# Holding back two kinds of transfer on one DMA queue until a unit's turned inputs are issued

## The chip, the cores and the metric

The kernel runs on one core of one Trainium2 chip. The metric is the time of one execution in device microseconds (us): the median of three runs. Beside it there is one execution taken by the hardware profiler, from which the trace and all its rows come.

## The reference

The reference applies the same two layers twice to one sequence of 2048 tokens with 576 channels, in bf16.

```python
def _layernorm(x, axis=-1, eps=1e-5):
    m = jnp.mean(x, axis=axis, keepdims=True)
    v = jnp.var(x, axis=axis, keepdims=True)
    return (x - m) / jnp.sqrt(v + eps)
...
    def _A_ref(q, k, v, shift_k, ssm_k, ssm_D):
...
        for t in range(ks):                      # ks = 4 taps
            k_shift = k_shift + k_pad[:, t:t + S, :] * shift_k[:, ks - 1 - t][None, None, :]
        kv = k_shift * v
...
        y = y + kv * ssm_D[None, None, :]        # y: causal convolution of kv with the filter ssm_k, by FFT
        return q * y

    def _B_ref(x, w_gate, w_up, w_down):
        return (_gelu(x @ w_gate) * (x @ w_up)) @ w_down

    x = A_q
    x = x + _A_ref(_layernorm(x, axis=-1), A_k, A_v, A_shift_k, A_ssm_k, A_ssm_D)
    x = x + _B_ref(_layernorm(x, axis=-1), B_w_gate, B_w_up, B_w_down)
    x = x + _A_ref(_layernorm(x, axis=-1), A_k, A_v, A_shift_k, A_ssm_k, A_ssm_D)
    x = x + _B_ref(_layernorm(x, axis=-1), B_w_gate, B_w_up, B_w_down)
    return x
```

The hidden width of the feed-forward layer B is 4608. The convolution's result y does not depend on x, so it is computed once and used in both layers A, where it multiplies the normed x (the gate).

## The kernel before

**Units and passes.** The 2048 tokens are four chunks of 512. A unit is one feed-forward layer on one chunk. There are eight, in this order: units 0 and 1 are the first layer on chunks 0 and 1, units 2 and 3 the second layer on chunks 0 and 1, units 4 to 7 the same on chunks 2 and 3. Passes over the weights hold the units [0], [1, 2], [3, 4], [5, 6], [7]. Each pass goes through the hidden width in three phases of 1536 columns, and in a phase it visits its units one after the other. A visit is 216 gate/up matmuls (line 1581; unit 0's first visit uses line 1506) with a GELU on ACT (line 1585) and a product on DVE (line 1586), and then 96 down matmuls (line 1601) in four accumulators, one for each block of 128 tokens. DVE adds these to the residual `x_c` (lines 1632 and 1637). Three buffers of PSUM serve gate/up pairs and down accumulators alike.

**A unit's input.** The gate/up matmuls need the normed x turned, channels on partitions: the tile `xnT`. For each block of 128 tokens a normed tile `xn` is made, on DVE (`norm_v`, lines 1265 and 1267) or on ACT (`norm`, line 1257), and put on the list `xn_made` with the time at which the planner expects it. `spreads` takes it from there and issues two DMA transposes from SP's queue (`spread`, line 1290), which write the block's columns of `xnT`. `xn_done[ui]` counts a unit's blocks; a unit has `RT` = 4. For unit 1 the norms of blocks 0, 2 and 3 are made on DVE, that of block 1 on ACT; for units 2 to 7 all are made on ACT. The small steps of each norm run on POOL (lines 1185, 1200, 1201, 1205) and its sum of squares on ACT (line 1193). `nq` holds norms that ACT is still to make.

**Weights.** Gate and up weights come in groups of four blocks of 128 hidden columns, three buffers (`load_wgu`, lines 1147 to 1149: three transfers on SP's queue), down weights in halves of a phase, three buffers (`load_wd`, line 1157, SP too). `when_due` puts a load with its due time on the list `due`; `weights` issues what is on it.

**The convolution beside it.** The class `Conv` computes y for chunks 2 and 3 while the units run. Its filter is turned first: `turn(b)` issues four DMA transposes of the filter from DRAM, one at a time, on SP's queue (line 429, tile `hb`), and later a write of the turned chunk to DRAM from POOL's queue (line 434, `Td`). `filt(b)` loads it from there (POOL, line 448, tile `hT`) and transforms it (PE line 289, ACT line 292, DVE lines 252 to 265). `step(b)` loads k and v for the chunk (POOL, lines 171 and 176), forms their product with the taps (DVE, lines 189 to 199), transforms it and multiplies. All these loads stand on one list, `conv.L`, which is worked off in its order by `run_loads`: `turn(2)`, `turn(3)`, `filt(2)` and its `step`, and so on. A piece of a turn is held for as long as `conv.turning()` is true.

**The order.** The program is written out in one pass over the visits, with a planner's clock: `t.pe`, `t.act` and `t.dve` are expected times. Between two pairs of gate/up matmuls, and between down matmuls, `fill` is called. It calls `weights`, then `conv.run_loads`, then `spreads`, and after these gives DVE, ACT, POOL and PE the steps of convolution and norms that fit the time left. What is issued on an engine stays in this order. SP's queue therefore carries weights, filter turns and the turns of `xnT` in the order in which `fill` came to them, and an entry that waits holds the ones behind it.

The test that holds weights back is in `weights`, and the one that holds the filter's turns is set just ahead of the visits:

```python
            near = (xn_made or nq) and xn_done.get(1, 0) < RT
            if near and due[0][0] > t.pe + HOLD:
                break
...
        conv.tight, conv.turning = chained, lambda: bool(xn_made or nq)
```

`HOLD` is 14 us. `nq` is filled only by norms that ACT makes, and `xn_made` is empty again as soon as `spreads` has issued what it holds.

Of the kernel before, what the change touches and what calls it, by code (L numbers as in the profile page):

```python
# [26 lines left out]
RT = BS // P  # L27
# [1062 lines left out]
def ssm_geglu_kernel(ctx, tc, A_q, A_k, A_v, A_shift_k, A_ssm_k, A_ssm_D, B_x, B_w_gate, B_w_up,  # L1090
# [45 lines left out]
    conv = Conv(spare, tc, ctx, t, A_k, A_v, A_shift_k, A_ssm_k, A_ssm_D, ident, psp, cpsp, ypool)  # L1136
# [32 lines left out]
    aq, nq = deque(), deque()  # L1169
# [115 lines left out]
    xn_made = deque()  # L1285
# [14 lines left out]
    xnT_of, xn_done = {}, {}  # L1300
# [32 lines left out]
    def when_due(when, load, n):  # L1333
        due.append((when, len(due), load, n))
        due.sort(key=lambda d: d[0])

    def weights():

        while due:
            near = (xn_made or nq) and xn_done.get(1, 0) < RT  # L1340
            if near and due[0][0] > t.pe + HOLD:
                break
            _, _, load, n = due.pop(0)
            load(n)
# [6 lines left out]
    def fill(limit, tensor, conv_first):  # L1351
        weights()
        conv.run_loads()
        spreads()
        while True:
            if conv_first:
                if not (conv.run_v(limit) or run_vq(limit)):
                    break
            else:
                done = run_vq(limit)  # L1360
                if done is None or not (done or conv.run_v(limit)):
                    break
        while run_aq(min(limit, t.pe + 2.3)):
            pass
        conv.flush(t.pe)
        if tensor and (hurry() or t.pe > conv.last + (CHAINED if chained() else 0.0)):
            for _ in range(3):
                if not conv.run_p():
                    break

    with tc.manual_schedule():
# [155 lines left out]
        def wanted():  # L1527
            need = vq[0][0] if vq else (None,)
            kind = conv.Pq[0][3] if conv.Pq and len(conv.Pq[0]) > 3 else None
            if isinstance(kind, tuple):  # L1530
                return kind[1:] >= LATE
            return kind is not None and need[0] == "y2" and need[1:3] not in conv.y_at
        now = lambda: wanted() or hurry() and (t.pe > 60.0 or conv.fresh > 0)
        conv.tight, conv.turning = chained, lambda: bool(xn_made or nq)
        visits = []
        for pi, us in enumerate(passes):
            visits += [(pi * NP + ph, ph, ui, k == 0, k == len(us) - 1)
# [1 line left out]
        for wb, ph, ui, first, final in visits:  # L1539
# [17 lines left out]
            if first and wb > 0:  # L1557
                when_due(t.pe + FP * C_GU, load_wd, 2 * wb + 1)
                when_due(t.pe + FP * C_GU + 35.0, load_wd, 2 * wb + 2)
            weights()  # L1560
            xnT = xnT_of[ui]
            end = ph == NP - 1
# [81 lines left out]
@with_exitstack  # L1644
def kernel(
    ctx: ExitStack,
    tc: tile.TileContext,
    A_q: bass.AP,
    A_k: bass.AP,
    A_v: bass.AP,  # L1650
    A_shift_k: bass.AP,
    A_ssm_k: bass.AP,
    A_ssm_D: bass.AP,
    B_x: bass.AP,
    B_w_gate: bass.AP,
    B_w_up: bass.AP,
    B_w_down: bass.AP,
    out: bass.AP,
):
    ssm_geglu_kernel(tc, A_q, A_k, A_v, A_shift_k, A_ssm_k, A_ssm_D, B_x, B_w_gate, B_w_up,  # L1660
                     B_w_down, out)
# [30 lines left out]
```

## Time and profile before

| | us |
|---|---|
| median of three runs | 923.30 (923.29 to 923.41) |
| profiled execution, its time | 923.42 |
| its span, first to last instruction | 921.5 |
| PE busy in the span | 909.2 (99%) |
| DVE, ACT, POOL busy | 577.1, 322.1, 160.8 |

Two groups of matmuls fill PE: gate/up (line 1581) with 543.0 us and down (line 1601) with 292.2 us. The profile in 40 slices has the three lines that show how even this is; each digit is a slice of 23 us in tenths, and the lowest line is the granted clock of PE.

```profile
PE   8999998999999999999999999999999999999998
DVE  7988977369898886596598997452333335432332
PEclk9999999899999999999999999999999999999999
```

The eighth slice (161 to 184 us) is the only one behind the start in which the clock is not full. Unit 1's first visit begins there.

In the rows of the trace that follow, PE is the matmul engine and PEld its weight loads, DVE the vector engine, ACT the scalar engine, POOL the general engine and SP the engine that issues most DMA; SPq is SP's queue. "L1581" is line 1581 of the kernel. A row of the timeline has the start, the duration, the engine, line and operation, what is written from what, and how often; rows of one kind in a row are merged.

### The profile page before, as it was taken

How to read it: one execution, taken by the hardware profiler on the slowest of the kernel's cores; microseconds unless marked ns; L12 is line 12 of the kernel's file. 1: busy time of each engine (PE TensorE's matmuls, PEld its weight loads, DVE VectorE, ACT ScalarE, POOL GpSimd, SP SyncE). 2: the span in 40 equal slices, each digit the busy share in tenths (PEclk: the TensorE clock that was granted, in tenths of full speed). 3: DMA queues.
4: the chain of work that ended last, by engine and by line, in shares of the span. 5: the costliest groups of instructions: out<-in, count | busy, mean ns of one | idle time of the engine just before them, and what ended most of it. 6: DMA issues, size and time to landing. Idle time of an engine off the chain costs nothing.

```text
span 921.5 us, 19273 instructions
## 1 busy us (share of the span) xinstructions
PE 909.2 (99%) x8198; PEld 530.6 (58%) x8198; DVE 577.1 (63%) x982; ACT 322.1 (35%) x602; POOL 160.8 (17%) x334
## 2 busy tenths in 40 slices
PE   8999998999999999999999999999999999999998
PEld 6786545465564664655645646546546556556555
DVE  7988977369898886596598997452333335432332
ACT  6843245433215136362223233561221224421211
POOL 3512024202115013150012301220000003100000
PEclk9999999899999999999999999999999999999999
DMA  9998978819636808866643921960820821967720
GB/s 247 333 257 250 201 180 161 209 68 233 179 105 130 250 1 129 197 141 153 145 138 92 227 71 31 194 138 1 155 78 2 153 80 22 170 170 165 144 66 26
DMA packets 128955, 131.14 MB, mean 142 GB/s; under 512 B 43619, under 2 KB 120676, under 8 KB 128869
## 3 DMA queue, kind: packets, MB, share of 16 engines
q1 hardware_dynamic: 119232, 93.47, 48.0%
q0 software_dynamic: 9632, 36.43, 12.3%
q8 instruction: 64, 1.05, 0.5%
q14 instruction: 23, 0.18, 0.1%
q10 hardware_dynamic: 4, 0.01, 0.0%
HBM read 108.35 MB, written 11.80 MB: 130 GB/s over the span
## 4 chain that ended last, share of the span: by engine, by line
PE 96%; DVE 1%; ACT 1%; DMA 1%; POOL 0%; issue 0%; ACTq 0%; POOLq 0%; DVEq 0%
PE gu L1581 59%; PE dn L1601 30%; PE gu L1506 3%; PE ps L214 1%; PE cps L389 1%; PE cps L289 1%; DMA xnT<-xn 1%; PE ps L389 0%; PE ps L289 0%; DVE wx L936 0%; PE cps L214 0%; ACT junk L1193 0%; PE cps L873 0%; DVE wx L939 0%; POOL rstd L1201 0%
## 5 line engine op out<-in xcount | busy, mean ns | idle before, releaser
L1581 PE MATMUL gu<-xnT,wgu 64*128 64x512 bf16 x4968 | 543.0, 378 | 5.1 <-DMA xnT<-xn 5.1
L1581 PEld LDWEIGHTS <-wgu 64*128 64x128 bf16 x4968 | 242.4, 94 | 298.8 <-issue 13.3
L1585 ACT ACTIVATE ga<-gu 128x512 f32<-128x512 f32 x276 | 164.6, 597 | 489.0 <-PE gu L1581 480.6
L1586 DVE TENSOR_TENSOR hT<-ga,gu 128x512 bf16<-128x512 f32 x276 | 189.4, 686 | 220.9 <-ACT ga L1585 218.6
L1601 PE MATMUL dn<-wd,hT 128*128 128x288 bf16 x2304 | 292.2, 287 | 0.0
L1601 PEld LDWEIGHTS <-hT 128*128 128x128 bf16 x2304 | 223.3, 98 | 65.7 <-issue 9.3
L1637 DVE TENSOR_TENSOR x_c<-x_c,dn 128x576 f32<-128x576 f32 x64 | 48.1, 752 | 58.1 <-PE dn L1601 58.1
L1185 POOL TENSOR_SCALAR nm<-s 128x1 f32<-128x1 f32 x60 | 21.8, 363 | 274.3 <-DVE x_c L1632 203.2
L1193 ACT ACTIVATE junk<-x_c,nm 128x576 bf16<-128x576 f32 x48 | 36.9, 770 | 29.7 <-POOL nm L1185 28.1
L1201 POOL TENSOR_TENSOR rstd<-ve,neghalf_t 128x1 f32<-128x1 f32 x62 | 41.8, 673 | 5.2
L529 POOL DMA_DIRECT2D hr<-Hd x32 | 17.5, 546 | 116.2 <-DVE prod L348 112.0
L1200 POOL TENSOR_SCALAR ve<-ss 128x1 f32<-128x1 f32 x62 | 24.5, 395 | 56.0 <-ACT junk L1193 55.8
L1257 ACT ACTIVATE xn<-x_c,nb,rstd 128x576 bf16<-128x576 f32 (+1 forms) x50 | 29.8, 644 | 6.0 <-POOL nb L1205 5.9
L1623 DVE TENSOR_TENSOR ob<-x_c,dn 128x576 bf16<-128x576 f32 x15 | 11.3, 754 | 23.2 <-PE dn L1601 20.7
L1506 PE MATMUL gu<-xnT,wgu 64*128 64x256 bf16 x432 | 24.6, 270 | 0.0
L292 ACT COPY eo<-cps 128x576 f32<-128x576 f32 x26 | 16.6, 637 | 19.6 <-PE cps L289 14.9
L349 DVE TENSOR_TENSOR prod<-prod 128x576 bf16<-128x576 bf16 x48 | 22.0, 458 | 1.7
L1506 PEld LDWEIGHTS <-wgu 64*128 64x128 bf16 x432 | 20.8, 94 | 3.3 <-issue 0.9
L404 POOL DMA_DIRECT2D out_dram<-ob x12 | 6.7, 557 | 81.7 <-DVE ob L1623 61.2
L1235 DVE SCALAR_TENSOR_TENSOR x_c<-g_t,rstd,x_c 128x576 f32<-128x576 f32 x16 | 13.0, 814 | 9.2 <-POOL rstd L1201 9.2
L252 DVE SCALAR_TENSOR_TENSOR eo<-eo 128x576 f32<-128x576 f32 x20 | 14.8, 753 | 5.8 <-ACT eo L292 5.8
L587 DVE TENSOR_TENSOR zs<-sum,prod 128x576 f32<-128x576 bf16 x24 | 18.1, 754 | 0.3
(168 smaller groups left out, 557.2 us busy)
## 6 DMA issues: line engine op xcount, KB each, us to landing
wgu<-in_B_w_gate_dram SPq DMA_DIRECT2D x45, 576.0 KB, 5.9
wd<-in_B_w_down_dram SPq DMA_DIRECT2D x30, 864.0 KB, 6.8
wgu<-in_B_w_up_dram SPq DMA_DIRECT2D x45, 512.0 KB, 8.0
hr<-Hd POOLq DMA_DIRECT2D x32, 288.0 KB, 5.4
kr<-Kd POOLq DMA_DIRECT2D x24, 288.0 KB, 6.1
Kd<-kc POOLq DMA_DIRECT2D x12, 288.0 KB, 5.2
k<-in_A_k_dram POOLq DMA_DIRECT2D x3, 1008.0 KB, 11.6
wgu<-in_B_w_up_dram SPq DMA_DIRECT2D x45, 64.0 KB, 7.6
```

The lines of the kernel that those rows point to most:

```text
L349: nc.vector.tensor_tensor(out=dst, in0=pr[:, 0, :], in1=pr[:, 1, :], op=ALU.subtract if part == 0 else ALU.add)
L1185: nc.gpsimd.tensor_scalar(out=v["nm"][:], in0=v["s"][:], scalar1=-1.0 / D, scalar2=None, op0=ALU.mult)
L1193: nc.scalar.activation(out=junk[:], in_=get_x(), func=ACT.Square, bias=v["nm"][:, 0:1], accum_out=v["ss"][:])
L1200: nc.gpsimd.tensor_scalar(out=ve[:], in0=v["ss"][:], scalar1=1.0 / D, scalar2=EPS, op0=ALU.mult, op1=ALU.add)
L1201: nc.gpsimd.tensor_tensor(out=v["rstd"][:], in0=ve[:], in1=neghalf_t[:, 0:1], op=ALU.pow)
L1257: nc.scalar.activation(out=xn[:, lo:hi], in_=x_c[c][:, j, 0:hi - lo], func=ACT.Identity, scale=v["rstd"][:, 0:1], bias=v["nb"][:, 0:1])
L1506: nc.tensor.matmul(pair[:, s, e * 256:(e + 1) * 256], lhsT=w[r0:r0 + HK, k, gi * P:(gi + 1) * P], rhs=xnT[r0:r0 + HK, blk_of[k], tok], sta ...
L1581: nc.tensor.matmul(pair[:, s, :], lhsT=w[r0:r0 + HK, k, gi * P:(gi + 1) * P], rhs=xnT[r0:r0 + HK, b, :], start=(k == 0), stop=(k == NKC - 1))
L1585: nc.scalar.activation(out=ga[:], in_=pair[:, 0, :], func=ACT.Gelu_apprx_tanh)
L1586: nc.vector.tensor_tensor(out=hT[:, fi, :], in0=ga[:], in1=pair[:, 1, :], op=ALU.mult)
L1601: nc.tensor.matmul(part[h][:, h, 0:HW], lhsT=hT[:, fi, at * P:(at + 1) * P], rhs=wd[2 * wb + fi // WT][:, fi % WT, h * HW:(h + 1) * HW], s ...
L1637: nc.vector.tensor_tensor(out=xh, in0=xh, in1=acc[:, :, 0:HW], op=ALU.add)
```

## The change

A function `turns_near` is added. It is true while there is a made norm not yet turned or a norm that ACT is still to make, as before, and also from the first issued turn of unit 1 (when `xnT_of` has its tile) until its fourth block has been issued. It takes the place of the old expression in both tests: in `weights` it holds back weights whose due time is more than `HOLD` ahead, and as `conv.turning` it holds the pieces of the filter's turn.

```diff
+    def turns_near():
+
+        return bool(xn_made or nq) or 1 in xnT_of and xn_done.get(1, 0) < RT
+
     def weights():
 
         while due:
-            near = (xn_made or nq) and xn_done.get(1, 0) < RT
+            near = turns_near() and xn_done.get(1, 0) < RT
             if near and due[0][0] > t.pe + HOLD:
                 break
             _, _, load, n = due.pop(0)
...
-        conv.tight, conv.turning = chained, lambda: bool(xn_made or nq)
+        conv.tight, conv.turning = chained, turns_near
```

No operation, tile or transfer is added or taken away. Lines of the kernel behind line 1336 move down by four.

## The prediction

> **What bounds the kernel now.** The summary of the chain that ended last comes first, then the table of who waited for whom on PE.
>
> ```profile
> PE 96%; DVE 1%; ACT 1%; DMA 1%; POOL 0%; issue 0%; ACTq 0%; POOLq 0%; DVEq 0%
> PE gu L1581 <- DMA xnT<-xn: 5.1, 1, 5.1
> PE cps L873 <- DVE full L851: 1.2, 1, 1.2
> ```
>
> PE is the chain. Behind the start-up it stands still once: 5.1 us in one piece, for the turned norms `xnT` that the gate/up matmuls of L1581 read. The chain in order of time says where (start, us):
>
> ```profile
> 163.43 25.62 PE gu L1581 x216
> 189.05 0.35 PE dn L1601 x2
> ...
> 202.87 23.41 PE gu L1581 x216
> ```
>
> This is the first stage of unit 1. Unit 0's last down matmul ends at 158.36, unit 1's first one starts at 163.43. The same 216 matmuls take 25.62 us here and 23.41 in the next stage, so 2.21 us more are lost behind the wait. The table by stretches (granted clock is the third number from the end) says why:
>
> ```profile
> 158.40:160.90 2.50, 0.00 (x0) 0.00 (x0) 1.55 (x5) 1.18 (x3) 1.09 (x4) 1.00 1.13 199
> 160.90:163.40 2.50, 0.00 (x0) 0.01 (x1) 0.00 (x0) 0.56 (x2) 1.63 (x5) 0.51 1.19 271
> 163.40:167.60 4.20, 4.17 (x20) 1.83 (x22) 0.00 (x0) 0.05 (x1) 0.19 (x1) 0.50 1.06 248
> 167.60:189.00 21.40, 21.40 (x199) 10.79 (x196) 9.77 (x16) 12.03 (x23) 4.90 (x12) 1.00 0.72 195
> ```
>
> 2.5 us into the wait the clock falls to half, and it stays there for 4.2 us of matmuls. Last, the timeline of SP's queue, which issues the turns (L1290; two to a token block, four blocks):
>
> ```profile
> 143.51 5.96 SPq L1290 DMA_TRANSPOSE xnT<-xn  x4
> 149.58 0.64 SPq L1147 DMA_DIRECT2D wgu<-in_B_w_gate_dram  x1
> 150.26 1.02 SPq L1148 DMA_DIRECT2D wgu<-in_B_w_up_dram  x1
> 151.33 0.63 SPq L1149 DMA_DIRECT2D wgu<-in_B_w_up_dram  x1
> 152.01 1.27 SPq L429 DMA_TRANSPOSE hb<-in_A_ssm_k_dram  x1
> 153.37 6.47 SPq L1290 DMA_TRANSPOSE xnT<-xn  x4
> ```
>
> Blocks 1 and 2 go out, then three weight transfers and one turn of the filter, then blocks 3 and 4. Their inputs, made on DVE, were there before:
>
> ```profile
> 150.26 0.57 DVE L1265 TENSOR_SCALAR xn<-x_c,nm,rstd 128x576 bf16<-128x576 f32 x1
> 150.87 0.18 DVE L1267 COPY xn<-xn 128x64 bf16<-128x64 bf16 x1
> 150.97 0.57 DVE L1265 TENSOR_SCALAR xn<-x_c,nm,rstd 128x576 bf16<-128x576 f32 x1
> 151.57 0.18 DVE L1267 COPY xn<-xn 128x64 bf16<-128x64 bf16 x1
> ```
>
> Block 3 is ready at 151.05, block 4 at 151.75. Read in quarter-microsecond stretches, the DMA moves weights from 150.75 to about 157, then the held filter turn and block 3 (until 159.6). Then comes POOL's load of the turned filter (L448, issued at 157.59), and only from 161.75 to 164 come block 4's small packets with those of the next filter turn. Block 4's turns, issued at 157.31 and 158.57, land 6.0 and 5.1 us later: 163.3 and 163.7, which is when PE goes on.
>
> **The change, part by part.** The order of the two programs' instructions differs in this way. On SP, L1147 to L1149 and the filter turn that stood between blocks 2 and 3 now stand behind block 4, and the second filter turn still comes behind unit 2's first block. On POOL, L448 moves behind eight small steps of two token blocks' norms and the load L1162. On PE nothing but one filter step (L289), at some 198 us, moves ahead by two down matmuls; on DVE the filter and `kv` steps of that stretch move with it. No instruction is added or removed.
>
> *Blocks 3 and 4.* SP now waits for DVE instead, until 151.05, and nothing else stands behind that wait that PE needs soon. From 151.1 there are four turns. At the quietest pitch (143.51 to 144.79, 1.28 us) the last is issued at 151.1 + 3 x 1.28 = 154.9. At the slowest pitch of blocks 1 and 2 (146.30 to 147.97, 1.67 us) it is 151.1 + 3 x 1.67 = 156.1. From issue to landing the turns of blocks 1 and 2 took 2.5, 2.6 and, the last one with weights right behind it, 4.1 us. So the last turn lands between 154.9 + 2.5 = 157.4 and 156.1 + 4.1 = 160.2. PE is free at 158.36 and reaches the rows of that last turn after two matmuls, at 158.6. The wait that is left is 0 to 1.6 us; I take 0.4, nearer the quiet end: the issue by the quiet pitch and the landing by the row of 4.1, as again weights come right behind (154.9 + 4.1 = 159.0). Gain: 5.06 - 0.4 = 4.66 us, bounds 3.5 and 5.06.
>
> *The clock.* The clock fell 2.5 us into the idle time; what is left is shorter on both bounds, so the 2.21 us are gained whole. The Trainium skill (TensorE: Matmul & The Clock Gate, "What's actually happening") has the clock halved after an idle window of about 3.4 us and back after about 3.4 us of work. By it the loss is half of 3.4, 1.7 us, and the sum 0.5 us smaller; the trace has 4.2 us of slow work and an earlier fall, and I go by the trace.
>
> *The weights held back.* The three transfers are issued at about 156.3 to 157.8 rather than at 149.58. They fill the third of unit 1's groups, first read by its ninth pair of matmuls, 8 x 1.95 us (23.41/12) behind 158.6: 174.2. Landed 7.7 us behind issue (the slowest of the old three), they are there by 167. Cover: eight pairs of matmuls; cost nothing.
>
> *The filter turns.* The held one goes out at about 159, the second near 163 (159.89 before). Behind them: the write of the turned filter (POOL L434, 177.30 before, behind the norms in POOL's order), the load of `k` (182.35, which waited 4.2 us for that write), then L189 on DVE (198.55). All of this but the DMA is tied to the norms and to PE, and comes some 7 us earlier. The load of L448 moves from 157.59 to about 164 and lands 5.7 us later, at 170; its reader L289 comes at 189.24 - 7.3 = 182. Cost nothing; cover 12 us.
>
> *Sum.* 4.66 + 2.21 = 6.87 us off the profiled execution's 923.42 us (span 921.5 and 1.9 around it): 916.55. The median of the runs is 0.12 lower than the profiled one, so 916.4. With the bounds: 916.0 to 917.6.
>
> **The rivals.** (a) *The norms of unit 2 take the place of the wait.* In the old run ACT, POOL and DVE worked through the norms of unit 2 while PE stood. Now they mix with the GELUs. From the durations: ACT's squares end at 161.46, so the first GELU ends at 162.1 and its product on DVE at 162.8; PE needs that buffer for its fourth pair at 164.4. The `xn` of L1257 (from 162.7, 1.2 us) holds the second GELU until 164.5 and its product until 165.2, needed at 166.3. Slack 1.6 and 1.1 us. Against it: the slack is positive at both places and POOL's new load ahead of a small step costs only 0.65. For it: these are chains over three engines. If it strikes, PE loses 0.5 to 2 us: 917 to 918.5.
>
> (b) *The turns were never slow because of the weights.* Block 3 waited behind them, but block 4's packets came late though weights had ended by 157. If turns run at their own pace whatever is around them, block 4 keeps its 6.0 and 5.1 us: issued at 153.7 and 154.9 it lands at 160.0, a wait of 1.4, inside the bounds; with an issue as slow as the one at 154.64 (2.57 us) it is 161.3, a wait of 2.7, and some of the clock loss comes back: 5.06 - 2.7 = 2.4 gained, plus 0 to 2.2, so 919 to 921. Against it: blocks 1 and 2 moved within a microsecond of their issue. By the Trainium skill's window of 3.4 us (same section) a wait of 2.7 would cost no clock; the trace, which lost it at 2.5, is kept.
>
> (c) *Slower: `k` comes late.* The held filter turns delay the write L434, that the load of `k`, and L189 stands on DVE ahead of the products that free PE's buffers. The first L189 now comes behind the second product of unit 2's stage, at 207.7 - 7.3 = 200; `k` is due at 171 (write) + 5.05 + 11.6 (its load to landing) = 188. The chain would have to slip 12 us before PE feels it, and 12 + 7 = 19 us before the kernel is slower than 923.4; each microsecond beyond costs one, say 925. Nothing in the old trace slips so.
>
> (d) *The change does nothing.* The order of SP excludes it: the two blocks move ahead.
>
> **How the numbers follow.** Forecast 0.78, (a) 0.11, (b) 0.07, (c) and anything else that makes it slower 0.03, (d) and the like 0.01. The time is 916.4. The forecast's own bounds are 916.0 to 917.6; (a) reaches 918.5. I take 915.7 to 918.6, the lower end 0.3 under the bound for a drift in the runs; what is left out is most of (b), (c) and a little more. About 0.2% (1.8 us) is what can be told from no change: faster 0.95, same 0.02, slower 0.03.
>
> **What would show it.** In PE's waits the line of 5.1 us is gone or under 1.6; the clock stands at 1.00 from 158 to 170, and the 216 matmuls of unit 1 take 23.4 us. SP shows eight L1290 before L1147, the last ending before 157. L289 and L189 wait for nothing. A wait of L1581 for DVE between 162 and 172 would be (a), a landing of block 4 past 160.5 would be (b), a wait of DVE for `k` near 200 (c). An unchanged span with the wait gone would prove the reading of the chain wrong.

## The result, and the profile after

| | before | after |
|---|---|---|
| median, four runs each | 923.36 us (923.29 to 923.46) | 916.12 us (915.88 to 916.32) |
| ratio, 95% interval | | 0.9921 [0.9904, 0.9939] |
| profiled execution, span | 923.42, 921.5 | 916.32, 914.3 |

The kernel became 0.8% faster. The table of who waited for whom on PE, in the changed kernel (us in total, times, longest), has lost the line of 5.1 us; what is left belongs to the start-up:

```profile
PE cps L873 <- DVE full L851: 1.2, 1, 1.2
PE ps L886 <- ACT sx L888: 0.7, 1, 0.7
```

The chain in order of time (start, us) passes from unit 0's last down matmuls into unit 1 without a gap:

```profile
146.55 11.87 PE dn L1605 x96
158.41 23.42 PE gu L1585 x216
```

Unit 1's first stage starts at 158.41 instead of 163.43 and takes 23.42 us instead of 25.62. The down matmuls ahead of it start 0.05 us later than before (146.55 against 146.50). So the wait that is gone is 5.02 + 0.05 = 5.07 us, and with the 2.20 us of the faster stage it is 7.27 us; the spans differ by 7.2. The clock, in the table by stretches (third number from the end):

```profile
158.40:160.90 2.50, 2.50 (x25) 1.13 (x26) 1.62 (x5) 0.99 (x3) 1.31 (x3) 1.00 1.03 229
160.90:163.40 2.50, 2.50 (x26) 1.15 (x24) 1.42 (x3) 1.76 (x5) 1.84 (x6) 1.00 1.14 206
163.40:167.60 4.20, 4.20 (x42) 1.87 (x40) 3.46 (x6) 3.45 (x8) 2.75 (x6) 1.00 1.19 294
```

Where 4.20 us held 20 matmuls at half clock, they now hold 42. SP's timeline shows the reason:

```profile
143.56 12.71 SPq L1290 DMA_TRANSPOSE xnT<-xn  x8
156.37 0.64 SPq L1147 DMA_DIRECT2D wgu<-in_B_w_gate_dram  x1
157.05 0.63 SPq L1148 DMA_DIRECT2D wgu<-in_B_w_up_dram  x1
157.73 0.63 SPq L1149 DMA_DIRECT2D wgu<-in_B_w_up_dram  x1
158.41 1.28 SPq L429 DMA_TRANSPOSE hb<-in_A_ssm_k_dram  x1
```

All eight turns stand ahead of the weights. The last one is issued at 155.01 and lands 2.5 us later, at 157.5, 0.9 us before PE asks for it.

### The profile page after: what moved, and what is told of

It reads as the page before. It is cut to its first block, busy times and chain, and to the rows that moved or that the text cites. A ratio compares the mean times of both kernels' runs of the same rounds, so it can differ in the third digit from the quotient of the medians.

```text
span 914.3 us, 19277 instructions
## 1 busy us (share of the span) xinstructions
PE 907.3 (99%) x8198; PEld 528.2 (58%) x8198; DVE 577.3 (63%) x982; ACT 321.8 (35%) x602; POOL 160.6 (18%) x334
## 4 chain that ended last, share of the span: by engine, by line
PE 98%; DVE 1%; ACT 1%; issue 0%; DVEq 0%; ACTq 0%
PE gu L1585 59%; PE dn L1605 31%; PE gu L1510 3%; PE ps L214 1%; PE cps L389 1%; PE cps L289 1%; DVE wx L936 0%; PE ps L389 0%; PE ps L289 0%; PE cps L214 0%; PE cps L873 0%; DVE wx L939 0%; ACT junk L1193 0%; PE xps L1403 0%; DVE v L930 0%; PE ps L950 0%
## 5 line engine op out<-in xcount | busy, mean ns | idle before, releaser
L1585 PEld LDWEIGHTS <-wgu 64*128 64x128 bf16 x4968 | 239.5, 94 | 294.4 <-issue 5.9
L1510 PEld LDWEIGHTS <-wgu 64*128 64x128 bf16 x432 | 20.8, 94 | 3.4 <-issue 0.7
```

Source lines behind the costliest of these rows:

```text
L1510: nc.tensor.matmul(pair[:, s, e * 256:(e + 1) * 256], lhsT=w[r0:r0 + HK, k, gi * P:(gi + 1) * P], rhs=xnT[r0:r0 + HK, blk_of[k], tok], sta ...
L1585: nc.tensor.matmul(pair[:, s, :], lhsT=w[r0:r0 + HK, k, gi * P:(gi + 1) * P], rhs=xnT[r0:r0 + HK, b, :], start=(k == 0), stop=(k == NKC - 1))
```

## The experiments

The two clauses of the change were tried one by one, then the clock's part and the one transfer on the other queue that crossed the turns. Each run had the kernel before beside it on the same chip (medians of 13 runs): 923.13 us for the weights alone, the filter's turns alone, PE kept busy and POOL's load moved away, and 923.77 us, on a second chip, for the other three.

**The weights alone.** The filter's hold is the old one:

```diff
-        conv.tight, conv.turning = chained, turns_near
+        conv.tight, conv.turning = chained, lambda: bool(xn_made or nq)
```

> The changed kernel with the new test in the weights alone; the filter's turn is held as before, so that one of its pieces is issued between blocks 2 and 3. My theory: the 1.15 MB of weights between the blocks made the wait, and the filter piece fits into the time in which SP waits for block 3 (149.5 to 151.1) and costs the turns behind it little. No wait of PE, clock 1.00, 916.1 us, at most 916.6. Rival (turns are slow whatever is around them): 919 to 921. Rival (the filter piece is half of the cost): 919 to 920.

Measured: 916.04 us (915.72 to 916.20), ratio to before 0.9918 [0.9903, 0.9933]; PE does not wait. SP's timeline:

```profile
143.15 5.97 SPq L1290 DMA_TRANSPOSE xnT<-xn  x4
149.17 1.90 SPq L429 DMA_TRANSPOSE hb<-in_A_ssm_k_dram  x1
151.17 5.16 SPq L1290 DMA_TRANSPOSE xnT<-xn  x4
156.43 0.64 SPq L1147 DMA_DIRECT2D wgu<-in_B_w_gate_dram  x1
```

In this execution everything up to here comes 0.42 us earlier than in the changed kernel (the down matmuls start at 146.13 against 146.55), and block 3's norm ends at 150.69:

```profile
150.51 0.18 DVE L1267 COPY xn<-xn 128x64 bf16<-128x64 bf16 x1
```

So the filter's piece fits almost into the time in which SP waits for block 3: the turns behind it start at 151.17, some 0.4 to 0.5 us after they could have. That is taken out of the slack of 0.9 us ahead of unit 1 and costs no time. One clause of the change brings all of its gain, and the filter piece on its own costs nothing here. Both rivals fall.

**The filter's turns alone.** Weights are tested as before:

```diff
-            near = turns_near() and xn_done.get(1, 0) < RT
+            near = (xn_made or nq) and xn_done.get(1, 0) < RT
```

> The other half: weights as before, the filter's turns held by the new test. POOL's load of the turned filter (L448) moves with them. My theory: block 3 is issued at 152.0 and its packets wait for the weights until 157; the third turn's issue is held up until then; block 4 lands at 160 to 160.8. PE waits 1.6 to 2.4 us and the clock, which fell 2.5 us into the old wait, stays full or nearly: 918 to 919 us. If the weights did nothing to the turns, there is no wait: 916.1. If only the weights matter and the filter's turns nothing at all: 923.3.

Measured: 917.65 us (917.46 to 917.94), 0.9937 [0.9920, 0.9953]. That is a little under the 918 to 919 expected. PE waits 1.7 us, the clock stays full. From PE's waits and SP's timeline:

```profile
PE gu L1585 <- DMA xnT<-xn: 1.7, 1, 1.7
```

```profile
151.25 0.63 SPq L1149 DMA_DIRECT2D wgu<-in_B_w_up_dram  x1
151.98 6.28 SPq L1290 DMA_TRANSPOSE xnT<-xn  x4
158.31 1.26 SPq L429 DMA_TRANSPOSE hb<-in_A_ssm_k_dram  x1
```

Block 3's first turn, issued at 151.98, needs 6.3 us to land. SP issues the third turn over 2.29 us instead of 1.2, until 156.94; by the quarter-microsecond reading that is when the last weight packets have gone. With neither a filter piece nor POOL's load among the turns, the weights make a wait of 1.7 us. Most of this run's gain over the kernel before is not the filter's turn, though: POOL's load L448 moved with it (issued at 162.89 instead of 157.59), which a run below tells apart, and a wait of 1.7 us keeps the clock.

**PE kept busy in the old wait.** The old wait is filled with matmuls whose result is not read:

```diff
+            if wb == NP and ui == 1:
+                idle = cpsp.tile([P, 2, 512], F32, tag="cps", name="idle")
+                for _ in range(22):
+                    nc.tensor.matmul(idle[:, 0, :], lhsT=ident[:], rhs=..., start=True, stop=True)
             for fi in range(FP if wb else 0):
```

> The kernel before, with 22 matmuls of 128x512 whose result nobody reads put on PE ahead of unit 1's first gate/up matmul (22 x 0.216 = 4.75 us of the old wait of 5.06). My theory: the wait stays, but PE's clock does not fall, and the 216 matmuls take 23.4 us: 923.3 - 2.2 = 921.1 us. If the slow start had another reason (weights or buffers late): 923.3.

Measured: 921.27 us (921.01 to 921.68, ten runs), 0.9978 [0.9968, 0.9987], and the granted clock 1.00 in each. The chain in order of time has unit 1's first stage at nearly its full speed, though its input still lands late (163.15):

```profile
162.97 23.49 PE gu L1585 x216
```

The difference to the kernel before beside it is 923.13 - 921.27 = 1.86 us. So the slow start of unit 1 was the clock and not late weights or buffers, and about 2 us of the change's 7 come from it.

**Half of them.** The same with `range(11)`.

> The kernel before with 11 idle matmuls (2.4 us) ahead of unit 1 instead of 22, so that PE stands still for 2.6 us behind them. The old clock fell 2.5 us into the wait, and where the wait was 2.8 us in two pieces it stayed full in one execution of four. If the fall needs 2.5 us at the most, some or all executions lose clock: 922 to 923.3 us. If it needs 3.4 us (the figure that the Trainium skill gives, TensorE: Matmul & The Clock Gate), none does: 921.2 us.

Measured: 921.90 us as a median of ten, 0.9986 [0.9977, 0.9996], but spread from 921.11 to 924.44. PE stands still for 2.5 us in the profiled execution (from 160.59 to 163.06), which kept its clock. Five of ten executions report a mean clock of 1.00 and took 921.1 to 921.4; the other five report 0.996 or 0.998 and took 922.4 to 924.4. Only the profiled execution shows how long PE stood; that it was about 2.5 us in the others is taken from the build, not measured. If so, 2.5 us is where the clock falls in some executions and not in others. The Trainium skill (TensorE: Matmul & The Clock Gate, "What's actually happening") calls the window free-running, which fits the scatter; that a whole idle window of about 3.4 us comes ahead of the fall does not fit the kernel before, where it fell some 2.5 us into the wait.

**POOL's load moved away.** In the kernel before, with SP's order untouched, L448 is held until unit 2's second block has been issued:

```diff
-        self.L.append((lambda: max(self.fwd_at.get(b - 1, NEVER), self.td_at.get(b, NEVER)), load))
+        self.L.append((lambda: max(self.fwd_at.get(b - 1, NEVER), self.td_at.get(b, NEVER), NEVER if self.held() else 0.0), load))
...
+        conv.held = lambda: xn_done.get(2, 0) < 2
```

> The kernel before, with POOL's load of the turned filter (L448, 0.59 MB, issued at 157.59) put behind the second block of unit 2 (about 174); SP's order is untouched. My theory: it stood between block 3 and block 4; without it block 4's packets move right behind block 3's, from 159.6, and it lands at 161 to 161.7. PE's wait shrinks from 5.06 to 2.8 to 3.4 us, part of the clock's loss stays: 920 to 921.7 us. If the load has no part in it: 923.3, with the wait at 5.06.

Measured: 920.25 us (918.89 to 920.73), 0.9962 [0.9947, 0.9976]. The profiled execution, at 918.89, is the fastest. Its PE waits come first, then the DMA issues of block 4's two turns (median us to landing at the end), and last the same two rows of the kernel before:

```profile
PE gu L1582 <- DMA xnT<-xn: 2.8, 2, 2.2
```

```profile
xnT<-xn SPq DMA_TRANSPOSE x1, 2.6
xnT<-xn SPq DMA_TRANSPOSE x1, 2.5
```

```profile
xnT<-xn SPq DMA_TRANSPOSE x1, 6.0
xnT<-xn SPq DMA_TRANSPOSE x1, 5.1
```

Block 4's turns, issued at 157.40 and 158.66 as in the kernel before (157.31, 158.57), land in 2.6 and 2.5 us instead of 6.0 and 5.1. The load on POOL's queue made 2.2 us of the old wait (5.06 - 2.84), and the weights with the filter's piece behind them 2.84. With the 1.7 us of the run of the filter's turns alone, the piece's part in the kernel before is 1.1 us: it counts only when it is itself stuck behind weights. These parts come from one profiled execution each, and PE reaches the wait up to 0.4 us earlier in one than in another (157.98 here, 158.36 before), so they are good to about that. The other three runs took 920.2 to 920.7 and report a clock of 0.998; they lost some of it, the profiled one did not.

**The load against quiet turns.** In the changed kernel, L448 is issued straight from `spreads`, when unit 1's third block (in a second run, its second) has been issued in the program's order:

```diff
+        if b == 2:
+            self.early = load
...
             xn_done[ui] = xn_done.get(ui, 0) + 1
+            if (ui, xn_done[ui]) == (1, 3):
+                conv.early()
```

> The changed kernel (no weights and no filter piece between the blocks) with POOL's load of the turned filter L448 issued about 153, just ahead of block 4's turns (153.7 and 155.0). In the kernel before, block 4's turns overlapped that load and took 6.0 and 5.1 us. Theory A: the load by itself holds the turns up: block 4 lands at 159.7 to 160.1, PE waits 1.1 to 1.6 us, 917.2 to 917.7 us. Theory B: it only hurts where turns are already queued behind weights: block 4 lands at 157.5 as in the changed kernel, no wait, 916.0.

Measured: 916.65 us (916.49 to 916.99), 0.9926 [0.9911, 0.9941]. POOL issued the load at 153.22 and SP block 4's last turn at 155.04. That turn's row among the DMA issues:

```profile
xnT<-xn SPq DMA_TRANSPOSE x1, 4.3
```

It landed at 159.4 instead of 157.5. PE started unit 1 0.44 us late, and after two matmuls it stopped once more until 159.42, right behind that landing. The table puts the first wait down to a step of DVE, which gate/up does not read; the input that was still under way is `xnT` (the landing of block 4's first turn is not in the trace). So the load alone, with no weights about, holds turns up: theory A in kind, about half of it in size. By quarter microseconds, no more than two small packets of SP's queue move from 154.5 to 156.75, while the load has the DMA to itself with 1 to 20 packets in a quarter.

> The same with the load issued about 149.5, ahead of block 3's turns (151.1 and 152.4). Theory A: block 3 takes 5 to 6 us, block 4 lands about 2 us later than in the changed kernel, at 159 to 160: 916.5 to 917.5 us. Theory B: 916.0.

Measured: 915.92 us (915.81 and 916.04), 0.9918 [0.9898, 0.9938]. Issued at 148.90, the load slows block 3's first turn to 3.4 us, less than theory A had. Block 4's last turn is issued only 0.1 us later than in the changed kernel (155.11 against 155.01) and lands in 2.5 us, and PE does not wait: block 3, there by 155.1, is not needed before unit 1 starts.

## Why the prediction was right

916.4 us had been forecast, 916.12 was measured.

- *Blocks 3 and 4.* The place and the mechanism held: with nothing between the blocks SP waits for DVE and issues the four turns by 156.3. The quiet pitch was the right end (last issue at 155.01, forecast 154.9). The wait left was 0, not 0.4: the landing was mis-sized. I had taken 4.1 us, from the one turn of block 2 with weights behind it, and the four turns landed like quiet ones (2.5 or 2.6 where the row is there), with weights right behind again. The weights had not made that row: in the changed kernel the same turn of block 2, issued at 148.00, takes 4.2 us, though SP issues nothing behind it until 151.13. What made it stays open. The forecast is 0.3 us too long, and this term is more than all of it.
- *The clock.* 2.21 us forecast, 25.62 - 23.42 = 2.20 measured, and 1.86 from the runs in which only the clock was kept. The estimate of 1.7 us that the prediction worked out from the Trainium skill's window (TensorE: Matmul & The Clock Gate, "What's actually happening") is below both; the trace was the better guide. That the clock "fell 2.5 us into the idle time" was read as if it were a fixed point. It is not: half of the executions built for about 2.5 us of idle time kept it.
- *The weights held back.* Issued at 156.37 to 158.36; of the two whose landing is in the trace the later is there at 165.1 (7.8 us from issue to landing at the slowest); forecast by 167, needed at 174. No wait, cost nothing.
- *The filter turns.* The second piece went out at 164.05 (forecast near 163), L448 at 163.31 (164), the write L434 at 171.90 (171) and the load of `k` at 178.72; DVE's first L189 began at 200.93 (200), behind a product and not behind `k`. Cost nothing.
- *The rivals.* (a) First product of unit 1's stage ended at 162.45 (forecast 162.8), the second at 164.87 (165.2); PE never waited for a buffer. (b) is settled by two runs: turns are quick when nothing crosses them, and what had kept block 4 after the weights was the filter's piece and then POOL's load. (c) L189 did not wait.

One thing the prediction did not separate: it gave the two clauses of the change one sum. The weights clause alone makes it all. The load L448 appears in the prediction as one of the things that block 4 stood behind; it was 2.2 us of the 5.06, and at its time it could only strike because the weights had pushed block 4 into its way: with the weights alone held back it is issued at 157.23, and PE does not wait.

## What to carry to other kernels

A transfer that an engine will wait for should not stand behind bulk on its queue, but what the bulk costs is not only its own time: here 1.7 us of weights became 5.06 by holding up a filter piece (1.1) and pushing the turns into another queue's load (2.2), and 7.3 by letting PE's clock fall. Read the queue in its order and the DMA in short stretches, and remove the first thing in the row; what stood behind it may cost nothing then. Where a wait of PE is about as long as the time after which its clock falls, shortening it below that is worth more than its length.

## What the runs showed of the hardware that had not been expected

A plain load on POOL's queue (0.59 MB) holds up DMA transposes that SP's queue has issued, even while it moves little: between 159.75 and 160.75 in the kernel before the DMA's share was under 0.85, falling to 0.18, and block 4's turns, issued at 157.31 and 158.57, still did not move. The profile counts the load on queue q0 and the turns on q1. In a quarter microsecond with both under way it shows q0 alone (packets, MB, share of 16 engines), at 160.25 in the kernel before and at 156.00 in the changed kernel with the load ahead of block 4:

```profile
q0 software_dynamic: 3, 0.01, 18.2%
q0 software_dynamic: 13, 0.06, 79.4%
```

With the load away block 4's turns took 2.5 and 2.6 us, with it 5.1 and 6.0, and the last one 4.3 in the changed kernel with no weights about. Why they stop was not tried.

PE's clock has no sharp threshold of idle time: the four executions of the kernel whose profile shows a wait of 1.7 us kept it, and five of ten built for about 2.5 us. The traces suggest what decides. In the kernel before PE stopped at 158.36; the clock fell at 160.97 and was back at 167.79, of which the table by stretches shows the end:

```profile
167.40:168.00 0.60, 0.60 (x8) 0.24 (x4) 0.00 (x0) 0.45 (x1) 0.00 (x0) 0.67 1.09 290
```

The half clock lasted 6.83 us, twice 3.41, and in the eight traces that record the clock every stretch at full clock is a whole number of the same 3.41 us (150.19 us is 44 of them, 904.53 us is 265). Counted in such steps, PE worked for only 0.8 us of the one that ended when the clock fell; in the three profiles that kept it through waits of 1.7, 2.5 and 2.2 + 0.7 us, PE worked for at least 1.7 us of every step. So the clock seems to depend on how an idle time falls on the steps, and not on its length alone. No run tested this.
